# y by 32-feature blocks on quarters of the array, the state update on halves, and one chain for both power tables

## The chip, the cores and the metric

One Trainium2 chip, one of its cores. The metric is device time in microseconds (us), the median of three runs: 607.88 us before the change (607.52 to 608.14). Engines: PE is TensorE (PEld its weight loads), DVE is VectorE, ACT is ScalarE, POOL is GpSimd, SP is SyncE, whose queue issues the transfers (SPq).

## The reference

Two blocks after one another. The first is a linear attention with a decaying state, for each of 4 x 8 (batch, head) pairs over 768 steps with 48 features:

```
cur   = (u * k_t) outer v_t
y_t   = r_t @ (state + cur)
state = w * state + k_t outer v_t
```

The second takes y as x of 3072 tokens by 384 features (8 heads x 48) and computes `((x @ w1) * (x @ w2)) @ w3 @ w_out`, with w1, w2 of 384 x 1024, w3 of 1024 x 1024 and w_out of 1024 x 384. All is float32; the weights of the second block come as float64, as two 32-bit halves of a 64-bit word each.

## The kernel before

**Units and chunks.** Time is cut into 6 chunks of 128 steps (`c`), and with 4 batches (`b`) this gives 24 units `n`, four to a chunk. Inside a unit the step-by-step recurrence becomes matrices. `scale(n)` multiplies k and r on DVE by tables of powers of w (`pnk`, `pnr`, L290 and L291), so that r times k over the features gives all decays at once, and computes the diagonal (u k r) with L297 to L299; ACT writes it into `AT`. `turn(n)` transposes the scaled k and r on PE (L310), and ACT copies them out (L312). `pairs(n)` multiplies them, head by head on 64 rows of the array (L321), and DVE writes the part above the diagonal into `AT` (L324). `output(n)` computes y: from the second chunk on it adds the state's part (L365, one 128-column matmul for each pair of heads, heads padded from 48 to 64 features) and the chunk's own part (L369, one matmul for a head on 64 columns of the array). `update(n)` computes k outer v (L392, one matmul for two heads, of which the diagonal halves count) and DVE adds it to the state and decays it with the array `keep`, which is also zero outside the diagonal halves (L399 and L400; L402 in the first chunk). The last chunk has no update.

**Where y goes.** Four pairs of heads, padded to 64, fill 4 x 128 rows, and x has 3 x 128. The first three pairs are copied straight into `xT` (L376). The last pair is copied to `y` (L375), and six small transfers (L380) put its rows into the holes of the other three, 16 rows each. The rows of w1 and w2 are loaded in the order that this leaves (`spread`), four transfers a piece (L133).

**The second block.** w1 and w2 come in twelve pieces of 128 x 512, converted from float64: ACT takes the absolute value of the high word (`power`, L244), six DVE operations follow (L245 to L252). Three buffers `raw` go round. w3 and w_out are converted in the same way, and `fold(j)` multiplies them into `w34` beforehand (L276 to L281), so that per chunk there remain `ab(c, j)` for 8 blocks j (L416 into `ps_a`, ACT's copy L418, L421 into `ps_b`, DVE's product L422) and `o(c, b)` (L427, L430, a transfer out). A float32 matmul is two instructions on PE, a transpose one.

**What sets the order.** The program is written as steps: for each unit `scale(n+1)`, `pairs(n)`, `turn(n+1)`, `output(n)`, `update(n)`, and between them as many entries of the chunk's list `beside[c]` as are due (L487). The list for chunk 0 is the first half of the pieces of w1 and w2; for chunk 1 the second half, beside the projection of chunk 0; for chunk 2 w_out and w3 beside the projection of chunk 1. From these steps a scheduler forms one queue for each engine, in which instructions run strictly in order; so an instruction that waits holds all behind it on its engine. It may place work of neighbouring steps before or behind one another.

**The start.** The powers of w are built by doubling: `up` (for r) on DVE, `down` (for k) on POOL, both from `wucol`, which a transpose on PE makes from `wu` (L164). They are transposed (L228) and copied (L230) before the first `scale` can write k and r.

The whole program exists twice, in a fast arm and in one for decays outside 0.6 to 1.6 (L497); the inputs take the fast one.

## Time and profile before

| | |
|---|---|
| median of the runs | 607.88 us |
| the profiled execution: its time, and its span | 606.07 us, 604.2 us |
| mean granted clock of PE | 0.991 |
| busy: PE, DVE, ACT, POOL | 554.2, 261.5, 172.6, 10.3 us |
| transfers | 88916 packets, 38.62 MB |
| y into the holes (L380) | 144 transfers of 8 KB, landing after 1.8 us |

The page cuts the span into 40 slices of 15.1 us and gives the busy share of each in tenths, 9 being 90% or more. A share over the whole span says little here: the start waits for loads and tables, the stretch up to about 133 us has conversions on DVE beside the recurrence, and after that PE is hardly ever idle. So the stretches are read apart. In the chain of waits each piece begins where the one before it ends; where all pieces belong to PE, their lengths are the price of PE's work.

### The profile page before, as it was taken

The page shows a single profiled execution, that of the slowest core. Times are in us where ns is not written, and L with a number is a line of the kernel's source. Part 1 is how long each engine was busy: PE and PEld are TensorE (multiplying, and loading weights), DVE is VectorE, ACT ScalarE, POOL GpSimd, SP SyncE. Part 2 cuts the span into 40 slices and gives each one's busy share as a digit, 9 for nine tenths or more (in the row PEclk, how much of TensorE's full clock was granted, in tenths as well). Part 3 has the DMA queues.
Part 4 walks back from the last instruction along what each step waited for, and adds up shares of the span by engine and source line. Part 5 has one row for each costly group of instructions (what it writes and reads, how often), then busy time and mean ns, then how long its engine had stood idle before and what let it go on. Part 6 is the DMA issues. An engine that isn't in the chain of part 4 may idle for free.

```text
span 604.2 us, 6718 instructions
## 1 busy us (share of the span) xinstructions
PE 554.2 (92%) x2441; PEld 321.0 (53%) x2441; DVE 261.5 (43%) x497; ACT 172.6 (29%) x423; POOL 10.3 (2%) x36
## 2 busy tenths in 40 slices
PE   0298987679999999999999999999999999999996
PEld 0277445344556656656555565565555555554453
DVE  3896578489996667765103131313121101001100
ACT  2465233334444334334012122131332211111100
POOL 2400000000000000000000000000000000000000
PEclk9999999699999999999999999999999999999999
DMA  8534862733754233420211111102100000000001
GB/s 158 109 76 96 158 123 58 142 83 82 202 150 104 85 97 88 112 63 17 52 40 29 27 43 28 42 17 52 31 16 14 16 17 16 18 36 0 1 14 43
DMA packets 88916, 38.62 MB, mean 64 GB/s; under 512 B 78761, under 2 KB 84266, under 8 KB 88874
## 3 DMA queue, kind: packets, MB, share of 16 engines
q1 hardware_dynamic: 88874, 38.10, 26.8%
q8 instruction: 21, 0.34, 0.2%
q14 instruction: 21, 0.17, 0.1%
HBM read 32.18 MB, written 4.72 MB: 61 GB/s over the span
## 4 chain that ended last, share of the span: by engine, by line
PE 86%; DVE 5%; SPq 4%; DMA 2%; ACT 1%; issue 1%; DVEq 0%; ACTq 0%
PE ps_o L427 21%; PE ps_a L416 20%; PE ps_b L421 20%; PE ps_w L280 7%; PE ps_y L369 4%; PE ps_a L321 4%; PE ps_y L365 3%; PE ps_s L392 3%; PE ps_rT L310 2%; PE ps_kT L310 2%; DMA rin<-in_r_dram 1%; SPq L380 1%; PE ps_w3T L276 1%; SPq L133 1%; DMA raw<-in_moe_w_dram 1%
## 5 line engine op out<-in xcount | busy, mean ns | idle before, releaser
L416 PE MATMUL ps_a<-xT,w 128*128 128x512 f32 x288 | 133.9, 600 | 4.2 <-DVE w L252 4.2
L421 PE MATMUL ps_b<-xT,w 128*128 128x512 f32 x288 | 133.8, 598 | 3.4 <-DVE w L252 2.5
L427 PE MATMUL ps_o<-w,abt 128*128 128x384 f32 x384 | 128.0, 490 | 0.0
L422 DVE TENSOR_TENSOR abt<-ps_b,a 128x512 f32<-128x512 f32 x48 | 33.1, 690 | 186.1 <-PE ps_b L421 169.1
L427 PEld LDWEIGHTS ps_o<-w,abt 128*128 128x128 f32 x384 | 71.8, 190 | 49.6 <-issue 2.3
L421 PEld LDWEIGHTS ps_b<-xT,w 128*128 128x128 f32 x288 | 54.3, 191 | 71.6 <-issue 63.4
L416 PEld LDWEIGHTS ps_a<-xT,w 128*128 128x128 f32 x288 | 52.9, 191 | 61.6 <-issue 52.2
L418 ACT COPY a<-ps_a 128x512 f32<-128x512 f32 x48 | 28.0, 584 | 140.6 <-PE ps_a L416 137.7
L304 ACT ACTIVATE AT<-ident,dg 128x128 f32<-128x128 f32 x192 | 58.9, 394 | 6.8 <-DVE dg L299 6.8
L430 ACT COPY osb<-ps_o 128x384 f32<-128x384 f32 x24 | 11.5, 478 | 119.6 <-PE ps_o L427 107.8
L280 PE MATMUL ps_w<-wo,w3T 128*128 128x384 f32 x128 | 43.0, 489 | 0.6 <-ACT w3T L277 0.5
L324 DVE COPY_PREDICATED AT<-later,ps_a 128x512 f32<-128x512 int32 x48 | 32.3, 721 | 18.8 <-PE ps_a L321 17.9
L321 PEld LDWEIGHTS ps_a<-rT,kT 64*128 64x128 f32 x384 | 25.3, 195 | 16.5 <-issue 8.4
L321 PE MATMUL ps_a<-rT,kT 64*128 64x128 f32 x384 | 31.4, 298 | 2.8 <-ACT rT L312 2.8
L280 PEld LDWEIGHTS ps_w<-wo,w3T 128*128 128x128 f32 x128 | 23.7, 190 | 16.0 <-ACT w3T L277 1.0
L244 ACT ACTIVATE power<-raw 128x512 f32<-128x512 f32 (+1 forms) x36 | 23.4, 653 | 25.2 <-DVE t L251 19.4
L369 PE MATMUL ps_y<-AT,vnat 128*64 128x128 f32 x384 | 28.8, 280 | 0.9 <-ACT kT L312 0.6
L392 PE MATMUL ps_s<-vnat,ks 128*128 128x128 f32 x160 | 24.3, 286 | 0.0
L369 PEld LDWEIGHTS ps_y<-AT,vnat 128*64 128x64 f32 x384 | 21.6, 136 | 4.9 <-ACT kT L312 0.8
L312 ACT COPY kT<-ps_kT 128x512 f32<-128x512 f32 x24 | 14.0, 584 | 34.9 <-PE ps_kT L310 34.9
L251 DVE SCALAR_TENSOR_TENSOR t<-raw,power 128x512 f32<-128x512 uint32 (+1 forms) x36 | 23.6, 656 | 0.3
L299 DVE TENSOR_REDUCE dg<-ruk 128x8 f32<-128x384 f32 x24 | 13.1, 547 | 24.3 <-ACT AT L304 24.2
(74 smaller groups left out, 382.6 us busy)
## 6 DMA issues: line engine op xcount, KB each, us to landing
raw<-in_moe_w_dram SPq DMA_DIRECT2D x16, 512.0 KB, 4.1
kin<-in_k_dram SPq DMA_DIRECT2D x24, 192.0 KB, 3.6
rin<-in_r_dram SPq DMA_DIRECT2D x24, 192.0 KB, 3.6
vnat<-in_v_dram SPq DMA_DIRECT2D x24, 192.0 KB, 3.4
raw<-in_moe_w_dram SPq DMA_DIRECT2D x24, 192.0 KB, 3.7
out_dram<-osb SPq DMA_DIRECT2D x24, 192.0 KB, 1.9
raw<-in_moe_w_out_dram SPq DMA_DIRECT2D x8, 384.0 KB, 3.3
xT<-y SPq DMA_DIRECT2D x144, 8.0 KB, 1.8
```

The costliest lines, as they stand in the source:

```text
L280: nc.tensor.matmul(ps, lhsT=w3T[:, kc, :], rhs=wo[kc], start=(kc == 0), stop=(kc == KF - 1))
L304: nc.scalar.activation(out=AT[n][:, i, p, :], in_=ident, func=COPY, scale=dg[:, h:h + 1])
L310: nc.tensor.transpose(ps[:, p, :], src[n % NS][:, 2 * p:2 * p + 2, :].rearrange("t h d -> t (h d)"), ident)
L321: nc.tensor.matmul(ps[i][:, p, :], lhsT=kT[n][rows(i), p, :], rhs=rT[n][rows(i), p, :], start=True, stop=True)
L324: nc.vector.copy_predicated(AT[n][:, i], later.bitcast(I32)[:, None, :].to_broadcast([C, NP, C]), ps[i])
L369: nc.tensor.matmul(ps[rows(i), p], lhsT=vnat[n % NV][:, 2 * p + i, :], rhs=AT[n][:, i, p, :], start=not c, stop=True, skip_group_check=True)
L392: nc.tensor.matmul(ps[:, p], lhsT=kk[:, 2 * p:2 * p + 2, :].rearrange("t h d -> t (h d)"), rhs=vnat[n % NV][:, 2 * p:2 * p + 2, :], start= ...
L416: nc.tensor.matmul(pa, lhsT=w1[:, q, js], rhs=xT[c][:, q, :], start=(q == 0), stop=(q == KM - 1))
L418: nc.scalar.copy(out=a, in_=pa)
L421: nc.tensor.matmul(pb, lhsT=w2[:, q, js], rhs=xT[c][:, q, :], start=(q == 0), stop=(q == KM - 1))
L422: nc.vector.tensor_mul(abt[c, j], pb, a)
L427: nc.tensor.matmul(po, lhsT=abt[c, j][:, b * C:(b + 1) * C], rhs=w34[:, j, :], start=(j == 0), stop=(j == KF - 1))
```

## The change

- **y in blocks of 32.** The 96 features of a pair of heads are three blocks of 32, and the twelve blocks of the four pairs land, four to a 128-row group, in three groups: this is x's own order, so `spread`, the copy to `y` and the six transfers of L380 are gone, and a piece of w1 or w2 is one transfer. A block uses 32 columns of the array. The state's part has 12 such matmuls per unit, the chunk's own part 16: a middle block holds features of two heads and takes two.
- **State.** `st` has 96 columns for a pair instead of 128. Each head's k outer v is a matmul on 64 columns of the array with 48 columns of v, all on the head's own rows. DVE adds the two halves apart (64 partitions each), and the decay is one multiply by the column `wc`, repeated; `keep` is gone.
- **Order.** `pairs(n+1)` is computed in unit n, ahead of `output(n)` and `update(n)`. There are two steps to a unit instead of five: `scale` and `turn` of the next unit; `pairs` of the next, `output` and `update`. The entries of `beside` come between these two.
- **Tables.** One array `both` holds the powers for k and for r, built by one chain on DVE; the decay column is loaded by two transfers instead of a transpose on PE. k and r share one array (`krin`, `krs`), so `scale` multiplies both in one instruction. An ACT instruction on one element (`warm`) stands at the very start.
- **Pieces of w1 and w2** are taken alternately, w1 and w2, instead of three of w1 and then three of w2.

The core of the diff:

```diff
     ab_pieces = ...
-                 for z in range(DF // PIECE) for dst, src in ((w1, moe_w1), (w2, moe_w2)) for q in range(KM)]
+                 for js in (slice(z * PIECE, (z + 1) * PIECE) for z in range(DF // PIECE))
+                 for q in range(KM) for dst, src in ((w1, moe_w1), (w2, moe_w2))]
...
-            for to, of in parts:
-                nc.sync.dma_start(out=raw[to], in_=src[of, cols])
+        nc.sync.dma_start(out=raw, in_=src)
...
         def output(n):
             ps = psM.tile([P, NP, C], F32, tag="m", name=f"ps_y{n}")
+            blocks = [(p, j, divmod(3 * p + j, P // Q)) for p in range(NP) for j in range(3)]
+            to = lambda q, g: ps[g * Q:(g + 1) * Q, q, :]
             if c:
-                for p in range(NP):
-                    nc.tensor.matmul(ps[:, p], lhsT=st[b][:, p].rearrange("x i e -> x (i e)"), rhs=rw[:, p], ...)
-            for p in range(NP):
-                for i in range(2):
-                    nc.tensor.matmul(ps[rows(i), p], lhsT=vnat[n % NV][:, 2 * p + i, :], rhs=AT[n][:, i, p, :], ...)
-            y = work.tile([P, C], F32, tag="y", bufs=3, name=f"y{n}")
-            nc.scalar.copy(out=y, in_=ps[:, NP - 1, :])
-            nc.scalar.copy(out=xT[c][:, :, bs], in_=ps[:, 0:KM, :])
-            for i in range(2):
-                for q in range(KM):
-                    at = i * PAD + q * HOLE
-                    nc.sync.dma_start(out=xT[c][i * PAD + D:(i + 1) * PAD, q, bs], in_=y[at:at + HOLE, :])
+                for p, j, (q, g) in blocks:
+                    nc.tensor.matmul(to(q, g), lhsT=st[b][:, p, j * Q:(j + 1) * Q], rhs=rw[:, p], ...)
+            at = (0, Q, PAD + D - Q)
+            parts = [(p, j, at[j], j // 2, pos) for p, j, pos in blocks]
+            parts += [(p, j, D, 1, pos) for p, j, pos in blocks if j == 1]
+            vv = vnat[n % NV].rearrange("t (p i) d -> t p (i d)", i=2)
+            for m, (p, j, x, i, (q, g)) in enumerate(parts):
+                nc.tensor.matmul(to(q, g), lhsT=vv[:, p, x:x + Q], rhs=AT[n][:, i, p, :], ...)
+            nc.scalar.copy(out=xT[c][:, :, b * C:(b + 1) * C], in_=ps[:, 0:KM, :])
...
         def update(n):
-            for p in range(NP):
-                nc.tensor.matmul(ps[:, p], lhsT=kk[:, 2 * p:2 * p + 2, :].rearrange("t h d -> t (h d)"),
-                                 rhs=vnat[n % NV][:, 2 * p:2 * p + 2, :], start=True, stop=True)
-            if fast:
-                if c:
-                    nc.vector.tensor_add(old, new, old)
-                    nc.vector.tensor_mul(old, old, by)
+            for p in range(NP):
+                for i in range(2):
+                    nc.tensor.matmul(ps[rows(i), p, 0:D], lhsT=kk[:, 2 * p + i, :], rhs=vnat[n % NV][:, 2 * p + i, 0:D],
+                                     start=True, stop=True)
+            for i in range(2):
+                own = st[b][rows(i), :, i * D:(i + 1) * D]
+                if fast and not c:
+                    nc.vector.tensor_mul(own, ps[rows(i), :, 0:D], wc[rows(i)].to_broadcast([PAD, NP, D]))
+                else:
+                    nc.vector.tensor_add(own, ps[rows(i), :, 0:D], own)
+            if fast and c:
+                nc.vector.tensor_mul(st[b], st[b], wc.to_broadcast([P, NP, PD]))
...
-                if n + 1 < NU:
-                    steps.append(lambda: scale(n + 1))
-                steps.append(lambda: pairs(n))
-                if n + 1 < NU:
-                    steps.append(lambda: turn(n + 1))
-                steps += [lambda: output(n), lambda: update(n)]
+                if n + 1 < NU:
+                    steps += [lambda: (scale(n + 1), turn(n + 1))]
+                steps += [lambda: (n + 1 < NU and pairs(n + 1), output(n), update(n))]
```

**PE, a unit of the third chunk.** Before, around y and update of unit 11 (the number behind a name is the scheduler's; a row is one matmul or, with x, so many):

```order
L416 MATMUL ps_a_6_1572<-xT_681,w_93 128x512 x3
L421 MATMUL ps_b_6_1578<-xT_681,w_94 128x512 x3
L310 MATMUL ps_kT_1583<-ident,ks_75 128x128 x4
L310 MATMUL ps_rT_1590<-ident,rs_77 128x128 x4
L365 MATMUL ps_y_1608<-rT_1430,st_85 128x128 x4
L369 MATMUL ps_y_1608<-AT_1364,vnat_74 64x128 x8
L392 MATMUL ps_s_1640<-vnat_74,ks_76 128x128 x4
L416 MATMUL ps_a_7_1648<-xT_681,w_93 128x512 x3
L421 MATMUL ps_b_7_1654<-xT_681,w_94 128x512 x3
```

After, around y and update of unit 9 (L299 the pairs, L347 and L355 y, L373 the update, L395 and L400 the projections, L287 the transposes):

```order
L299 MATMUL ps_a_0_1298<-rT_1262,kT_1255 128x128
L299 MATMUL ps_a_1_1299<-rT_1262,kT_1255 128x128
L347 MATMUL ps_y_1310<-rT_1107,st_78 32x128 x12
L355 MATMUL ps_y_1310<-AT_1086,vnat_69 32x128 x16
L373 MATMUL ps_s_1340<-vnat_69,krs_73 64x48 x8
L395 MATMUL ps_a_3_1364<-xT_659,w_91 128x512 x3
L400 MATMUL ps_b_3_1370<-xT_659,w_92 128x512 x3
L287 MATMUL ps_kT_1404<-ident,krs_73 128x128 x4
L287 MATMUL ps_rT_1411<-ident,krs_73 128x128 x4
```

The pairs of the next unit now stand directly ahead of y, and the update directly behind it; before, the pairs stand apart from y.

**ACT, in the second chunk**, where the second half of w1 and w2 is converted (`raw` in turn for pieces 9 to 12). Before:

```order
L244 ACTIVATE power<-raw_81 128x512
L375 COPY y_1029<-ps_y_1016 128x128
L376 COPY xT_681<-ps_y_1016 128x3x128
L418 COPY a_4_971<-ps_a_4_967 128x512
L244 ACTIVATE power<-raw_79 128x512
L312 COPY kT_995<-ps_kT_990 128x512
L312 COPY rT_1002<-ps_rT_997 128x512
L304 ACTIVATE AT_957<-ident,dg_953 128x128 x8
L418 COPY a_5_1009<-ps_a_5_1005 128x512
L244 ACTIVATE power<-raw_80 128x512
L375 COPY y_1162<-ps_y_1148 128x128
L244 ACTIVATE power<-raw_81 128x512
```

After, the last three of the twelve pieces:

```order
L223 ACTIVATE power<-raw_74 128x512
L397 COPY a_2_818<-ps_a_2_814 128x512
L223 ACTIVATE power<-raw_75 128x512
L359 COPY xT_659<-ps_y_879 128x3x128
L290 COPY kT_848<-ps_kT_843 128x512
L290 COPY rT_855<-ps_rT_850 128x512
L281 ACTIVATE AT_834<-ident,dg_830 128x128 x8
L223 ACTIVATE power<-raw_76 128x512
L397 COPY a_3_926<-ps_a_3_922 128x512
L397 COPY a_4_980<-ps_a_4_976 128x512
```

Before, three powers stand behind the copies of a_4 and a_5, which need the second half of w1; after, all stand ahead of the copy of a_4.

**DVE, from the first chunk to the second.** Before, where the fifth conversion begins (L245; L324 with AT_513 and AT_608 is the pairs of units 4 and 5):

```order
L324 COPY_PREDICATED AT_513<-later,ps_a_0_617 128x512
L298 TENSOR_TENSOR ruk_603<-ruk_603,ub 128x384
L324 COPY_PREDICATED AT_513<-later,ps_a_1_618 128x512
L299 TENSOR_REDUCE dg_604<-ruk_603 128x8
L399 TENSOR_TENSOR st_82<-ps_s_691,st_82 128x512
L400 TENSOR_TENSOR st_82<-st_82,keep 128x512
L324 COPY_PREDICATED AT_608<-later,ps_a_0_742 128x512
L324 COPY_PREDICATED AT_608<-later,ps_a_1_743 128x512
L245 SCALAR_TENSOR_TENSOR w_94<-power,raw_80 128x512
```

After, where the fifth and the sixth begin (L224; L302 with AT_492 is the pairs of unit 4):

```order
L224 SCALAR_TENSOR_TENSOR w_91<-power,raw_75 128x512
L380 TENSOR_TENSOR st_80<-ps_s_555,wn 64x4x48
L226 TENSOR_SCALAR t<-w_91 128x512
L380 TENSOR_TENSOR st_80<-ps_s_555,wn 64x4x48
L227 SCALAR_TENSOR_TENSOR w_91<-w_91,t 128x512
L269 TENSOR_TENSOR krs_73<-krin_68,pn 128x16x48
L229 TENSOR_SCALAR power<-w_91 128x512
L224 SCALAR_TENSOR_TENSOR w_92<-power,raw_76 128x512
L230 SCALAR_TENSOR_TENSOR t<-raw_75,power 128x512
L302 COPY_PREDICATED AT_492<-later,ps_a_0_525 128x512
```

The sixth conversion now begins before the pairs of unit 4; before, the fifth began behind those of unit 5.

## Rows read from the trace of the kernel before

**Rows 1.** The page: busy time by engine, and tenths in 40 slices.
```profile
PE 554.2 (92%) x2441; PEld 321.0 (53%) x2441; DVE 261.5 (43%) x497; ACT 172.6 (29%) x423; POOL 10.3 (2%) x36
...
PE   0298987679999999999999999999999999999996
...
PEclk9999999699999999999999999999999999999999
```
**Rows 2.** Busy time by stretch, with the granted clock and the transfers.
```profile
core 0: us, PE busy (x) PEld busy (x) DVE busy (x) ACT busy (x) POOL busy (x), PEclk, DMA share, GB/s
...
26.00:56.00 30.00, 25.34 (x225) 20.38 (x226) 25.27 (x48) 15.96 (x44) 0.00 (x0) 1.00 0.41 84
56.00:133.00 77.00, 61.85 (x334) 36.46 (x333) 52.38 (x94) 25.89 (x64) 0.00 (x0) 0.93 0.51 105
133.00:250.00 117.00, 115.58 (x499) 65.50 (x498) 93.76 (x186) 48.33 (x113) 0.00 (x0) 1.00 0.47 122
250.00:604.00 354.00, 349.23 (x1379) 196.93 (x1377) 75.64 (x125) 73.58 (x180) 0.00 (x0) 1.00 0.11 28
```
**Rows 3.** Who waited for whom, 56 to 133 us: us in total, times, longest.
```profile
DVE w L245 <- DMA raw<-in_moe_w_dram: 7.4, 2, 5.0
DVE AT L324 <- PE ps_a L321: 6.1, 1, 6.1
...
PE ps_a L416 <- DVE w L252: 4.2, 1, 4.2
...
PE ps_b L421 <- DVE w L252: 2.5, 3, 1.4
```
**Rows 4.** ACT in order of time: start, us, instruction [idle before <-releaser].
```profile
108.43 0.59 ACT L418 COPY a<-ps_a 128x512 f32<-128x512 f32 x1 [4.69 <-PE ps_a L416]
108.91 0.67 ACT L244 ACTIVATE power<-raw 128x512 f32<-128x512 f32 x1
```
**Rows 5.** SyncE's queue in order of time: start, us, issues.
```profile
85.56 1.71 SPq L133 DMA_DIRECT2D raw<-in_moe_w_dram  x4
...
96.85 1.72 SPq L133 DMA_DIRECT2D raw<-in_moe_w_dram  x4
98.67 4.40 SPq L380 DMA_DIRECT2D xT<-y  x6
106.50 1.71 SPq L133 DMA_DIRECT2D raw<-in_moe_w_dram  x4
```
**Rows 6.** The chain that ended last, steady part: start us, us, what.
```profile
348.06 0.89 PE ps_y L365 x8
348.95 1.02 PE ps_y L369 x16
349.97 5.36 PE ps_o L427 x16
355.33 0.89 PE ps_s L392 x8
...
361.37 1.09 PE ps_a L321 x16
...
516.82 20.64 PE ps_o L427 x64
```
**Rows 7.** DVE groups by line and shape: busy us, mean ns | idle before.
```profile
L297 DVE TENSOR_TENSOR ruk<-kin,rin 128x384 f32<-128x384 f32 x24 | 13.3, 554 | 21.6 <-DMA kin<-in_k_dram 15.2 <-DMA rin<-in_r_dram 6.3
...
L399 DVE TENSOR_TENSOR st<-ps_s,st 128x512 f32<-128x512 f32 x16 | 11.0, 689 | 22.3 <-PE ps_s L392 22.0
...
L400 DVE TENSOR_TENSOR st<-st,keep 128x512 f32<-128x512 f32 x16 | 11.0, 685 | 0.1
```
**Rows 8.** PE at the start, in order of time.
```profile
22.61 1.09 PE L228 MATMUL ps_pk<-ident,down 128*128 128x128 f32 x4 [18.31 <-POOL down L205]
...
27.83 1.12 PE L310 MATMUL ps_kT<-ident,ks 128*128 128x128 f32 x4 [3.28 <-DVE ks L290]
```

More of the change, by code (lines that the diff above doesn't have):

```diff
@@ L158 @@
                             skip_runtime_bounds_check_because="a comparison's result is 0 or 1")
-    wucol = const.tile([P, 2 * NP, 1], F32)
-    with tc.tile_pool(name="psW", bufs=1, space=PSUM) as psW:
-        ps = psW.tile([P, 2 * NP], F32, name="ps_wu")
-        nc.tensor.transpose(ps, wu.rearrange("a i d -> a (i d)"), ident[0:2 * NP, 0:2 * NP])
-        nc.vector.tensor_copy(out=wucol.rearrange("x a o -> x (a o)"), in_=ps)
     def program(fast):
@@ L177, in body @@
         psF = arm.enter_context(tc.tile_pool(name="psF", bufs=2, space=PSUM))
-        wn = tab.tile([P, LEVELS + 1, NP, 1], F32)
-        keep = tab.tile([P, NP, 2, PAD], F32)
-        pn = {}
+        for t in st:
+            nc.gpsimd.memset(t, 0.0)
         if fast:
-            nc.vector.tensor_scalar(wn[:, 0], wucol[:, 0:NP, :], W_LOW, W_HIGH, ALU.max, ALU.min)
-        else:
-            nc.vector.tensor_copy(out=wn[:, 0], in_=wucol[:, 0:NP, :])
-        for l in range(LEVELS):
-            nc.vector.tensor_mul(wn[:, l + 1], wn[:, l], wn[:, l])
@@ new lines, in body @@
+            wn = tab.tile([P, LEVELS + 1, 3 * NP, 1], F32)
+            nc.vector.tensor_scalar(wn[:, 0, 0:NP, :], wucol, W_LOW, W_HIGH, ALU.max, ALU.min)
+            for l in range(LEVELS):
+                nc.vector.tensor_mul(wn[:, l + 1, 0:NP, :], wn[:, l, 0:NP, :], wn[:, l, 0:NP, :])
+            nc.vector.reciprocal(wn[:, 0:LEVELS, NP:2 * NP, :], wn[:, 0:LEVELS, 0:NP, :])
+            nc.vector.tensor_copy(out=wn[:, 0:LEVELS, 2 * NP:, :], in_=wn[:, 0:LEVELS, 0:NP, :])
+            both = tab.tile([P, 2, NP, C], F32)
@@ L215, in body @@
+            natural = [both[:, g] for g in range(2)]
+        else:
+            wn = tab.tile([P, LEVELS + 1, NP, 1], F32)
+            nc.vector.tensor_copy(out=wn[:, 0], in_=wucol)
             pw = tab.tile([P, NP, C], F32)
@@ L267, in w3_weight @@
             js = slice(z * PIECE, (z + 1) * PIECE)
[L268 removed]
+            weight((w3n[j][:, js], moe_w3[j * P:(j + 1) * P, js]))
         def fold(j):
@@ L364, in output @@
-                for p in range(NP):
-                    nc.tensor.matmul(ps[:, p], lhsT=st[b][:, p].rearrange("x i e -> x (i e)"), rhs=rw[:, p],
-                                     start=(p == 0), stop=False, skip_group_check=True)
-            for p in range(NP):
-                for i in range(2):
-                    nc.tensor.matmul(ps[rows(i), p], lhsT=vnat[n % NV][:, 2 * p + i, :], rhs=AT[n][:, i, p, :],
-                                     start=not c, stop=True, skip_group_check=True)
+                for p, j, (q, g) in blocks:
+                    nc.tensor.matmul(to(q, g), lhsT=st[b][:, p, j * Q:(j + 1) * Q], rhs=rw[:, p],
+                                     start=(q == 0), stop=False, skip_group_check=True)
@@ new lines, in output @@
+            at = (0, Q, PAD + D - Q)
[3 more added lines that the diff above has]
+            for m, (p, j, x, i, (q, g)) in enumerate(parts):
+                nc.tensor.matmul(to(q, g), lhsT=vv[:, p, x:x + Q], rhs=AT[n][:, i, p, :],
+                                 start=(not c and m < P // Q), stop=True, skip_group_check=True)
@@ L472, in body @@
         turn(0)
+        pairs(0)
         for c in range(NCH):
```

140 lines of the change are left out of this document (57 added, 83 removed).

## The prediction

> **What bounds the kernel now.** I read the page first. TensorE is busy for 92% of the span, and its row of tenths shows where it is not: three slices at the start, and the slices around 100 to 135 us; the clock row has its one low digit there [rows 1]. The table of stages puts numbers on it: from 133 us on PE is busy for 115.58 of 117.00 us and 349.23 of 354.00, so there every microsecond of PE work is a microsecond of span; between 56 and 133 us it is busy for 61.85 of 77.00, at a mean granted clock of 0.93, while VectorE has 52.38 [rows 2]. So the change has two prices: PE work after 133 us, and waits before it.
>
> Next the waits between 56 and 133 us. PE waits longest for a converted weight piece (L252, 4.2 and 2.5 us), and DVE waits 7.4 us in front of L245 "for the raw weights" and 6.1 us for the pairs on PE [rows 3]. For the shorter of these two waits (7.4 - 5.0 = 2.4 us) the load is not to blame: three raw buffers go round, and the piece whose power is taken at 108.91 was issued at 85.56, before the loads at 96.85 and 106.50 for the two pieces behind it [rows 4, 5]. ScalarE shows the link that came last: the copy of the projection's result out of PSUM (L418) waits 4.69 us for PE and runs at 108.43, and the power of the weight piece (L244), queued behind it, starts at 108.91 [rows 4]. That is a ring: PE waits for DVE, DVE for ACT's power, that power for a copy, and the copy for PE. SyncE's queue is the second brake: six small DMAs per unit (L380) hold it for 4.40 us, behind them wait the loads of weights and of k, r, v [rows 5].
>
> Last the chain of waits in the steady part, where one unit's pieces stand with nothing between them [rows 6].
>
> **The change, part by part.** All sums are made against the profiled execution (606.07 us, of which 604.2 are span); the median of the runs is 1.81 us above it, and I add that difference again at the end.
>
> *y on quarters.* Eight whole-array instructions take 0.89 us (L365, L392), so one slot of 128 columns costs 0.111 us. The 16 half-array instructions of L321 take 1.09 us, and the work behind a visit to array parts is 0.20 us longer than it need be (5.36 us for 16 ps_o against 20.64/4 = 5.16) [rows 6]. Taking the same 0.20 off the entry of L321 leaves 0.89 us for 16 halves: two halves share one slot. Before, y costs 8 + 16/2 = 16 slots, 1.78 us per unit. After, it is 12 + 16 = 28 matmuls of two passes, 56 quarter instructions. If four share a slot as two halves do, that is 14 slots, 1.56 us (-0.22); if only two are ever beside each other, 56 x 0.0556 = 3.11 us (+1.33). The trace has no quarter. The nearest row is L321's, where every part of the array that exists is used; I take 1.60 (-0.18) and keep both ends.
>
> *State update on halves.* Four matmuls of 128 columns (0.89 us with their two passes, L392 [rows 6]) become eight on half arrays, 48 columns each: 16 instructions, two at a time. At the price of a half it stays 8 slots, 0.89 us; if it goes with the columns, 48/128 of that, 0.33. I take the middle, 0.60 (-0.29).
>
> *One visit.* Two visits per unit now cost 0.13 in (1.02 - 0.89, L369) and 0.20 out, 0.20 in (L321) and 0.20 out: 0.73 us [rows 6]. In the new order the pairs, y and the update follow one another, so PE enters and leaves once, 0.40, and changes its parts twice within. These inner changes are free at best (-0.33) and cost 0.20 each at worst (+0.07); as every change of parts in the rows costs 0.13 to 0.20, I take 0.15 each: -0.03. The Trainium skill, TensorEngine Tiling (Array Packing), section Key Properties, says that changing the tiling mode, and not only the tile, drains TensorE: by it 64-row to 32-column to 64-column are drains too, and "one visit" as such saves next to nothing. The trace's 0.13 to 0.20 us agrees for the changes from and to the whole array; the inner ones no run shows yet.
>
> Together -0.50 us for a unit with an update and -0.21 without. From 133 us on there are twelve and four of them: 6.0 + 0.8 = 6.8 us.
>
> *The front, 26 to 133 us.* DVE is busy for 25.27 + 52.38 = 77.7 of these 107 us [rows 2], and ten of the twelve conversions of w1 and w2 lie in it. The merged scale and the smaller update (two adds on 64 partitions at some 0.29 and one multiply at 0.55 for 0.69 + 0.69 [rows 7], estimates from the elements) take about 2 us off. Without a wait DVE would be through at 26 + 76 = 102 us; that is one bound (31 us gained). PE has 61.85 us of work from 56 us on, less about 2 for four units and 2 for the clock: it can't stand where it now stands at 133 before 56 + 58 = 114; that is the binding bound, 19 us. The other end is no gain at all. What speaks for most of it: in the new order ACT computes the power of all twelve pieces ahead of the copy of a_4, the first result that needs the second half of the weights, so the ring is cut; the 6 x 24 DMAs of L380 are gone, and a raw piece is one issue in place of four; and the six pieces that the first half of the projection needs stand inside chunk 0 on DVE, in place of four and a bit. I take 16 of the 19. What is late next is DVE: in 133 to 250 us it is busy for 93.76 of 117.00 us [rows 2], so a PE that comes 16 us early meets w_out and w3 conversions ahead of the scale of the next units; I price that at 4 us (bounds 0 and 16). Net 12 us.
>
> *At nothing:* the start. The power table of k ends on POOL and PE waits 18.31 us for it; then another 3.28 us pass until the first scaled k, because DVE does a weight piece between [rows 8]. In the new order one DVE chain makes both tables, with the same loads in front and again conversion steps in between; the early table load on ACT and one DMA for the decay column in place of a transpose are hidden behind these loads. It could be 1.5 us better or worse. The removed copies of y (L375) lie beside PE.
>
> Sum: 6.8 + 12 = 18.8 us off; 606.07 - 18.8 = 587.3, and with the 1.81 us to the median **589 us**.
>
> **Rivals.**
> 1. *Quarters run only two at a time* (slower). The two passes of a matmul go to the same quarter; if PE starts them in order and looks one ahead, two are beside each other, as in L321. Then y is 3.11 us: +1.33 - 0.29 - 0.03 = +1.01 per unit, 12.1 us for twelve, 5.2 for the last four, and the front keeps 12 - 4 x 1.5 = 6: 607.9 + 17.3 - 6 = 619 us. It decides below 2.5 quarters to a slot: 56 x 0.111 / 2.5 = 2.49 us, 0.89 more than I count, is over 20 units 17.8 of the 18.8 us. Against it: halves already use all that there is, two of two.
> 2. *Three at a time.* y is 56 x 0.111 / 3 = 2.07 us, +0.29, which the update gives back: steady part 0.7 us worse, front 12 - 4 x 0.47 = 10: 598.6 us. The Trainium skill, TensorE: Matmul & The Clock Gate, section Measured speedup vs the span model, has three column tiles at 2.38 times one; by that share four quarters would be 3.2 at a time, some 597 us. The trace shows 2.0 for two, no more.
> 3. *The front stays.* The waits of rows 3 change their names: PE in order behind pairs that are now computed a unit ahead, or DVE behind two more conversions in chunk 0. Then 6.8 and some 2 us of chunk 1 are left: 599 us. For it: DVE is the fuller engine until 250 us. Against: the ring on ACT is cut by order, not by luck.
> 4. *The front is gained whole* and the inner changes are free: 19 + 6.8 + 16 x 0.3 = 30 us, 578 us.
>
> **Chances.** Forecast 0.52 (its own range 582 to 596), rival 1 0.13, rival 2 0.13, rival 3 0.14, rival 4 0.08. The range takes in rivals 2 to 4 and part of the way to rival 1: 577 to 607. A change under 0.2% (1.2 us) can't be told from none. Faster: all but rival 1 and a little of rival 3, 0.82; slower 0.15; same 0.03.
>
> **What would show it.** Right: in the chain of the steady part y takes about 1.6 us for its 56 instructions, groups starting in fours; the update about 0.6; the extra on the work behind a visit appears once per unit; between 56 and 133 us PE is busy for over 90%, and the wait of L416 for a converted piece is short. Wrong: quarter instructions of 0.055 us apiece (rival 1), a wait of the scale or the transposes of units 8 to 11 for DVE of more than 5 us, or an idle PE around 100 us as now (rival 3).

## The result and the profile after

The changed kernel takes 569.23 us (569.16 to 569.48, four runs) beside 608.01 us for the kernel before: a ratio of 0.9364, 95% interval 0.9348 to 0.938. That is 38.8 us off. The forecast was 18.8 us off, 589 us, in a range of 577 to 607: the direction was right, the time lies below the range, and the gain is twice what was forecast.

The page of the kernel after: busy time by engine, then PE and its clock in 40 slices of 14.2 us, as in [rows 1].

```profile
PE 534.4 (94%) x3304; PEld 304.8 (54%) x3304; DVE 254.9 (45%) x495; ACT 169.2 (30%) x400; POOL 3.5 (1%) x17
...
PE   0388999999999999999999999999999999999996
...
PEclk9999999999999999999999999999999999999998
```

The holes around 100 to 135 us are gone, and with them the low clock digit. The profiled execution (569.27 us) has a span of 567.8 us, 36.4 less than before. PE's busy time fell by 554.2 - 534.4 = 19.8 us, its idle time by the other 16.6 (604.2 - 554.2 = 50.0 to 567.8 - 534.4 = 33.4).

The stages of the kernel after, with the columns of [rows 2]:

```profile
26.00:56.00 30.00, 25.47 (x351) 19.32 (x349) 28.57 (x54) 18.22 (x45) 0.00 (x0) 1.00 0.69 161
56.00:133.00 77.00, 76.90 (x578) 42.14 (x578) 76.38 (x158) 35.78 (x88) 0.00 (x0) 1.00 0.51 134
133.00:250.00 117.00, 116.58 (x842) 69.80 (x841) 83.37 (x155) 47.16 (x108) 0.00 (x0) 1.00 0.31 86
250.00:567.80 317.80, 312.66 (x1527) 171.18 (x1525) 52.14 (x83) 59.41 (x137) 0.00 (x0) 1.00 0.10 26
```

From 56 to 133 us PE is busy for 76.90 of 77.00 us at full clock, where it had 61.85 at 0.93, and DVE for 76.38 where it had 52.38. Behind it, from 133 to 250 us, DVE has less left to do (83.37 for 93.76), so nothing is given back. The waits of PE from 26 to 133 us (in total, times, longest; here the longest two) lie before 56 us; the 4.2 us for a converted piece and the 2.5 of [rows 3] have no successor:

```profile
PE ps_y L355 <- DVE AT L302: 1.5, 3, 1.1
PE ps_y L355 <- ACT AT L281: 1.3, 1, 1.3
```

How much earlier the front ends is read on PE at the first product of the fold (w_out with w3). Before:

```profile
179.80 2.42 PE L280 MATMUL ps_w<-wo,w3T 128*128 128x384 f32 x7
```

and after:

```profile
154.03 2.20 PE L259 MATMUL ps_w<-wo,w3T 128*128 128x384 f32 x6
```

25.8 us. The rest of the 36.4, 10.6 us, comes behind it, in the steady part, whose chain reads (start, us, what; compare [rows 6]):

```profile
280.62 1.09 PE ps_a L299 x16
281.71 0.79 PE ps_y L347 x24
282.50 0.87 PE ps_y L355 x32
283.37 0.60 PE ps_s L373 x16
283.98 2.77 PE ps_a L395 x6
286.75 2.58 PE ps_b L400 x6
```

The pairs cost what they did. y is 0.79 + 0.87 = 1.66 us for 56 quarter instructions, the update 0.61 with the gap behind it, and the whole-array work behind pays 2.77 - 2.58 = 0.19. One unit before: 0.89 + 1.02 + 0.20 + 0.89 + 1.09 + 0.20 = 4.29 us; after: 1.09 + 1.66 + 0.61 + 0.19 = 3.55. That is 0.74 less, and 0.46 less in a unit without update. For the twelve and four units that the prediction counts this makes 12 x 0.74 + 4 x 0.46 = 10.7 us. That it is next to the 10.6 is luck, for the two rows of the fold don't stand behind the same work: in the kernel after, PE has computed one unit more when it comes to the fold (the updates of eleven units, before of ten), some 3.5 us of work. At equal work 25.8 + 3.5 = 29.3 us come ahead of the fold and 7.1 behind it; the thirteen units left there, nine of them with an update, make 9 x 0.74 + 4 x 0.46 = 8.5, 1.4 more than that.

### The profile page after: what moved, and what is told of

It reads as the page before. It is cut to its first block, busy times and chain, and to the rows that moved or that the text cites. A ratio compares the mean times of both kernels' runs of the same rounds, so it can differ in the third digit from the quotient of the medians.

```text
span 567.8 us, 8077 instructions
## 1 busy us (share of the span) xinstructions
PE 534.4 (94%) x3304; PEld 304.8 (54%) x3304; DVE 254.9 (45%) x495; ACT 169.2 (30%) x400; POOL 3.5 (1%) x17
## 3 DMA queue, kind: packets, MB, share of 16 engines
q1 hardware_dynamic: 84082, 36.91, 25.0%
## 4 chain that ended last, share of the span: by engine, by line
PE 87%; DVE 7%; SPq 2%; issue 1%; ACT 1%; DMA 1%; ACTq 0%; DVEq 0%
PE ps_o L406 22%; PE ps_b L400 21%; PE ps_a L395 20%; PE ps_w L259 7%; PE ps_a L299 4%; PE ps_y L355 3%; PE ps_y L347 3%; PE ps_kT L287 2%; PE ps_s L373 2%; PE ps_rT L287 1%; PE ps_w3T L255 1%; SPq L109 1%; DMA krin<-in_r_dram 1%; DVE krs L269 1%; DVE AT L302 1%
## 5 line engine op out<-in xcount | busy, mean ns | idle before, releaser
L395 PE MATMUL ps_a<-xT,w 128*128 128x512 f32 x288 | 133.2, 597 | 0.0
L400 PE MATMUL ps_b<-xT,w 128*128 128x512 f32 x288 | 132.1, 593 | 0.1
L400 PEld LDWEIGHTS ps_b<-xT,w 128*128 128x128 f32 x288 | 54.4, 190 | 68.9 <-issue 64.3
L395 PEld LDWEIGHTS ps_a<-xT,w 128*128 128x128 f32 x288 | 53.1, 190 | 56.6 <-issue 50.9
L302 DVE COPY_PREDICATED AT<-later,ps_a 128x512 f32<-128x512 int32 x48 | 32.9, 731 | 30.7 <-PE ps_a L299 30.3
L299 PEld LDWEIGHTS ps_a<-rT,kT 64*128 64x128 f32 x384 | 25.4, 190 | 16.4 <-issue 9.4
L359 ACT COPY xT<-ps_y 128x384 f32<-128x384 f32 x24 | 11.4, 476 | 73.7 <-PE ps_y L355 73.5
L299 PE MATMUL ps_a<-rT,kT 64*128 64x128 f32 x384 | 30.7, 289 | 1.2 <-ACT rT L290 0.8
L355 PE MATMUL ps_y<-AT,vnat 128*32 128x128 f32 x768 | 28.3, 274 | 2.9 <-DVE AT L302 1.5
L355 PEld LDWEIGHTS ps_y<-AT,vnat 128*32 128x32 f32 x768 | 22.4, 110 | 4.5 <-DVE AT L302 2.5
L269 DVE TENSOR_TENSOR krs<-krin,pn 128x768 f32<-128x768 f32 x24 | 22.9, 957 | 0.6
```

What stands on the lines that cost most here:

```text
L269: nc.vector.tensor_mul(krs[n % NS][:, :, :, :D], kr, pn[:, :, :, :D])
L299: nc.tensor.matmul(ps[i][:, p, :], lhsT=kT[n][rows(i), p, :], rhs=rT[n][rows(i), p, :], start=True, stop=True)
L302: nc.vector.copy_predicated(AT[n][:, i], later.bitcast(I32)[:, None, :].to_broadcast([C, NP, C]), ps[i])
L355: nc.tensor.matmul(to(q, g), lhsT=vv[:, p, x:x + Q], rhs=AT[n][:, i, p, :], start=(not c and m < P // Q), stop=True, skip_group_check=True)
L395: nc.tensor.matmul(pa, lhsT=w1[:, q, js], rhs=xT[c][:, q, :], start=(q == 0), stop=(q == KM - 1))
L400: nc.tensor.matmul(pb, lhsT=w2[:, q, js], rhs=xT[c][:, q, :], start=(q == 0), stop=(q == KM - 1))
```

## The experiments

Theory Q: the front is held by SyncE's queue, in which the six small transfers of each unit and the four issues of each piece stand in order. Its rivals: the new order of steps (S), and the smaller work on PE and DVE (W).

**Run 1: after, with the five steps of before.**

```diff
-                    steps += [lambda: (scale(n + 1), turn(n + 1))]
-                steps += [lambda: (n + 1 < NU and pairs(n + 1), output(n), update(n))]
+                    steps.append(lambda: scale(n + 1))
+                steps.append(lambda: pairs(n))
+                if n + 1 < NU:
+                    steps.append(lambda: turn(n + 1))
+                steps += [lambda: output(n), lambda: update(n)]
```

> The changed kernel with the old five steps to a unit (scale, pairs of this unit, turn, output, update, with the projection's work between all of them). Theory S (the new order of steps freed the front): the waits between 56 and 133 us come back, PE is idle there for 10 us or more, 584 to 590 us. Theory Q (the transfers taken out of SyncE's queue freed it, and with them the scheduler placed ACT's powers early): the front stays, PE busy over 95% from 56 to 133 us; only the visits to array parts rise from 34 to 58, each unit some 0.2 us dearer: 573 to 576 us.

Measured 576.85 us (ratio 0.9504, 0.9479 to 0.953), 7.6 above after and just over Q's range. PE is busy for 540.6 us, 6.2 more, and idle for 34.2, 0.8 more: the new steps save PE's busy time (it goes to array parts 34 times instead of 58), not waits. From 56 to 133 us it is busy for 75.49 of 77.00 us: the front is free without them.

**Run 4: before, with the steps of after.**

```diff
-                    steps.append(lambda: scale(n + 1))
-                steps.append(lambda: pairs(n))
-                ...
-                steps += [lambda: output(n), lambda: update(n)]
+                    steps += [lambda: (scale(n + 1), turn(n + 1))]
+                steps += [lambda: (n + 1 < NU and pairs(n + 1), output(n), update(n))]
```

> The kernel before, with the new order of steps alone (pairs of the next unit ahead of output and update, two steps to a unit). Theory S: the front is freed, 585 to 592 us. Theory Q: the front's waits stay (ACT's powers still stand behind the copies of a_4 and a_5), only some exits from array parts go: 600 to 607 us.

606.61 us (0.9968, 0.9936 to 1.0001): no difference. S falls.

**Run 5: before, with the queue freed.**

```diff
-            y = work.tile([P, C], F32, tag="y", bufs=3, name=f"y{n}")
-            nc.scalar.copy(out=y, in_=ps[:, NP - 1, :])
-            ... nc.sync.dma_start(out=xT[c][i * PAD + D:(i + 1) * PAD, q, bs], in_=y[at:at + HOLE, :])   (x6)
     def spread(q):
-        ... four parts
+        return [(slice(0, P), slice(q * P, (q + 1) * P))]
```

> The kernel before with SyncE's queue freed and nothing else: the copy of pair 3's y and the six small transfers of each unit (L380) left out, and a piece of w1 or w2 loaded by one transfer instead of four (so the rows of pair 3 are missing from x, and the weights' rows are not in x's order: the output isn't the reference's). y stays on halves, the update on the whole array, the old steps. Theory Q (the queue held the front): after's front without its cheaper y, update and start; e1 shows 31.2 us with old steps, of these some 10.5 are the steady part, 2.6 the start and 2 the front's own cheaper PE work, so 16 are left: 590 to 594 us, PE busy over 90% of 56 to 133 us. Rival W (the front came from less work on PE and DVE in chunk 0, by merged scale, smaller update, quarters): 602 to 608 us, PE still near 62 us busy in 56 to 133.

578.93 us (0.9524, 0.947 to 0.9579): 28.4 us off, nearly twice what Q had expected, and W falls. PE runs the same 2441 instructions as before. The page's first row and three stages:

```profile
PE 546.2 (95%) x2441; PEld 318.2 (55%) x2441; DVE 258.0 (45%) x497; ACT 168.3 (29%) x399; POOL 9.9 (2%) x36
```

```profile
26.00:56.00 30.00, 28.57 (x236) 21.78 (x237) 27.93 (x53) 18.34 (x45) 0.00 (x0) 1.00 0.70 160
56.00:133.00 77.00, 77.00 (x392) 43.74 (x391) 77.00 (x159) 34.97 (x86) 0.00 (x0) 1.00 0.52 137
133.00:250.00 117.00, 116.45 (x563) 71.12 (x562) 81.81 (x147) 44.41 (x101) 0.00 (x0) 1.00 0.32 84
```

Span 576.9, 27.3 less than before: 19.3 us of idle time (50.0 to 30.7) and 8.0 us of busy time on the same instructions (554.2 to 546.2). PE and DVE are both full from 56 to 133 us. The first product of the fold runs at 151.89 us, 27.9 earlier than in the kernel before (179.80), with the same instructions ahead of it on PE: the whole gain lies in the front. With the six transfers the edit also takes their copy off ACT (L375, 24 times 0.27 us) and the projection no longer waits for them; run 6 keeps both. SyncE's queue shows what changed (start, us that the issues took, what). Before:

```profile
31.00 1.27 SPq L133 DMA_DIRECT2D raw<-in_moe_w_dram  x2
36.44 3.77 SPq L380 DMA_DIRECT2D xT<-y  x6
40.31 1.44 SPq L101 DMA_DIRECT2D vnat<-in_v_dram  x1
41.84 3.69 SPq L380 DMA_DIRECT2D xT<-y  x6
45.63 0.53 SPq L101 DMA_DIRECT2D vnat<-in_v_dram  x1
46.67 3.67 SPq L380 DMA_DIRECT2D xT<-y  x6
...
52.50 3.49 SPq L133 DMA_DIRECT2D raw<-in_moe_w_dram  x4
```

and in run 5:

```profile
29.90 0.65 SPq L124 DMA_DIRECT2D raw<-in_moe_w_dram  x1
...
35.97 0.53 SPq L124 DMA_DIRECT2D raw<-in_moe_w_dram  x1
...
43.02 0.34 SPq L124 DMA_DIRECT2D raw<-in_moe_w_dram  x1
```

The fifth piece is loaded at 29.90 (52.50 before), the seventh at 43.02: no block of six issues that must wait for y of its unit stands ahead of it.

**Run 6: before, with the pieces in one transfer; the six transfers stay.**

```diff
     def spread(q):
-        ... four parts
+        return [(slice(0, P), slice(q * P, (q + 1) * P))]
```

> The kernel before with the 12 pieces of w1 and w2 loaded by one transfer each instead of four (their rows then not in x's order, the output isn't the reference's); the six small transfers per unit stay. Theory Q4 (the 48 issues of the piece loads are what counts): nearly e5, 591 to 597 us. Theory Q6 (the 144 small transfers count, in whose shadow the loads stand): 603 to 608 us. Both alike: 598 to 603 us.

585.87 us (0.9633, 0.9562 to 0.9704): 21.4 of the 28.4 us come by the 36 issues less for twelve pieces, and 6.9 more when the 144 small transfers go too (run 5). Q4, and more of it than expected. What the small transfers alone give, with four issues to a piece left, was not run in the kernel before.

**Run 8: after, with the six small transfers.**

```diff
+            y = work.tile([P, C], F32, tag="y", bufs=3, name=f"y{n}")
+            nc.scalar.copy(out=y, in_=ps[:, KM - 1, :])
+            ... nc.sync.dma_start(out=z[i * PAD + D:(i + 1) * PAD, q, :], in_=y[at:at + 16, :])   (x6)
```

> The kernel after with only the six small transfers per unit back (a copy of 128x128 on ACT and six transfers into a tile that nobody reads). ACT's powers keep after's places. Theory Q4: 569 to 575 us, the transfers cost only what they delay k, r, v. Theory Q6: 600 to 640 us.

576.32 us (0.9484, 0.9429 to 0.954): 7.1 above after, the mirror of the 6.9, a little over Q4's range.

**Runs 2 and 7: after, with pieces in four transfers, with and without the small ones.**

```diff
-        nc.sync.dma_start(out=raw, in_=src)
+        for at, to in ((0, 48), (48, 64), (64, 112), (112, 128)):
+            nc.sync.dma_start(out=raw[at:to], in_=src[at:to])
```

> The changed kernel with the old load on SyncE's queue: each weight piece in four transfers again, and per unit one more copy on ACT and six small transfers into a scratch tile that nothing reads. Theory Q: the front's waits come back, PE idle by 10 us or more between 56 and 133 us, 582 to 592 us. Theory S: the transfers are hidden as long as PE has work, at most 572 us.

> The kernel after with only the 12 piece loads in four transfers each (36 issues more, some 16 us of SyncE by 0.43 us each). Theory Q4: most of e2's 74.6 us come back, 610 to 635 us, since in the program's order on ACT the powers of the w3 pieces then also fall behind the copies of the projection. Theory Q6: 569 to 576 us.

643.8 us (1.0607, 1.0574 to 1.064) and 590.79 us (0.9711, 0.9656 to 0.9767). Both miss, and both edits were heavier than their expectations say: they split all 36 pieces, w3 and w_out too, where the kernel before splits twelve. So they show that a longer queue costs more, slower than before even, but not the size for twelve. Nor do the two parts add: the issues alone cost 21.6 us (run 7), the small transfers alone 7.1 (run 8), both together 74.6 (run 2).

**Run 9: after, with the queue of before.**

```diff
-        nc.sync.dma_start(out=raw, in_=src)
+        for at, to in ((0, 48), (48, 64), (64, 112), (112, 128)) if any(piece is x for x in ab_pieces) else ((0, P),):
+            nc.sync.dma_start(out=raw[at:to], in_=src[at:to])
+            ... and the copy and six transfers of run 8
```

> The kernel after with exactly the queue of the kernel before: the 12 pieces of w1 and w2 in four transfers each (the second and the seventh run split all 36 pieces, w3 and w_out too, so they say more than was meant), and the six small transfers with the copy on ACT. Theory Q (the queue is the front, whatever else changed): the 28.4 us of the fifth run come back, 590 to 603 us. Rival O (the new order is more sensitive to the queue than the old one, as the second run's 643.8 us suggests): over 620 us. Rival N (the new order needs the queue less): under 582 us.

602.78 us (0.9904, 0.9876 to 0.9932): 33.6 us come back, 26.5 of them over run 8 by the 36 issues. (Unlike before, w1 and w2 still take turns, and nothing reads what the small transfers write.) From 56 to 133 us its row is like before's again, low clock and all:

```profile
56.00:133.00 77.00, 57.75 (x475) 30.89 (x474) 48.92 (x89) 25.68 (x65) 0.00 (x0) 0.91 0.52 101
```

Its idle time (599.3 - 546.6 = 52.7) is 19.3 over after's, the same 19.3 that run 5 took away. The queue is thus shown from both sides; everything else in the change is worth 1% while the old queue stands, and 9.7 us once it is free (578.93 in run 5, 569.23 after).

**Run 3: after, with the update on the whole array.**

```diff
-                for i in range(2):
-                    nc.tensor.matmul(ps[rows(i), p, 0:D], lhsT=kk[:, 2 * p + i, :], rhs=vnat[n % NV][:, 2 * p + i, 0:D], ...)
+                nc.tensor.matmul(ps[:, p], lhsT=kk[:, 2 * p:2 * p + 2, :]..., rhs=vnat[n % NV][:, 2 * p:2 * p + 2, :]..., ...)
```

> The changed kernel with the state update on the whole array again (four matmuls of 128 columns for two heads each; the diagonal halves are added). If the halves are what makes the update cheap (0.61 us with the change of parts, against 0.89 and an exit of 0.20 before it): 20 units x 0.28 us more, 574 to 576 us. If the 48 columns gain nothing and only the visit counts: within 1 us of the changed kernel.

573.75 us (0.9445), 4.5 over after; PE is busy for 539.0, 4.6 more. Over 20 units that is 0.23 us each for the halves.

**Run 10: after, with y's blocks sorted by quarter.**

```diff
-            blocks = [(p, j, divmod(3 * p + j, P // Q)) for p in range(NP) for j in range(3)]
+            blocks = sorted([...], key=lambda t: t[2][1])
...
```

> The kernel after with the blocks of y sorted by quarter, so that the matmuls of one quarter follow one another, three or four blocks of two passes each. If TensorE starts its instructions in order and neighbours must lie in different quarters: 56 x 0.111 = 6.2 us for y less the overlap at the changes, some +3.9 us for 20 units and +2.4 for four, 640 to 660 us. If it sorts them into quarters by itself: 568 to 573 us. If the four-fold share in y is not real and the whole gain lies elsewhere: also 568 to 573, but with y's time in the chain unchanged near 1.66 us.

591.14 us (0.9718, 0.9687 to 0.9749), between the two. The chain of one unit:

```profile
292.66 1.09 PE ps_a L299 x16
293.75 1.19 PE ps_y L347 x20
294.94 0.03 PE ps_y L355
294.97 0.08 PE ps_y L347 x2
...
295.27 1.21 PE ps_y L355 x28
296.48 0.60 PE ps_s L373 x16
```

y is 296.48 - 293.75 = 2.73 us, 1.07 more, which over 20 units is 21.4 of the 21.9. So the order over the quarters is what makes y 1.66, and four do run at once in after: 32 instructions in 0.87 us are 0.027 each, a quarter of a slot of 0.111; at that price the other 24 take 0.65 of their 0.79, and 0.14 is the entry into quarters. But sorted, it is still 0.049 each and not 0.11: within a quarter the records start 0.110 us apart, and the next quarter's first instruction starts 0.248 us after the first one of the quarter before, whose last three of six start only behind it. So, by these records, PE does not hold up a later instruction for another quarter behind them: in the chain L355 starts ahead of the last of L347, which stand before it in the program. To that extent PE's queue is not strictly in order.

**Runs 13 and 14: the power of the twelve pieces on DVE, in before and in run 9's kernel.** Run 5 leaves open how the queue costs its 28 us.

```diff
-            nc.scalar.activation(out=power, in_=hi.bitcast(F32), func=ABS)
+            if src is moe_w1 or src is moe_w2:
+                nc.vector.tensor_scalar(pb, hi, 0x7FFFFFFF, None, ALU.bitwise_and)
+            else: ...
```

> The kernel before with its queue and its steps as they are; only the power of the 12 pieces of w1 and w2 (|high word|, L244) is taken by VectorE, in front of its own conversion, and no longer by ScalarE. DVE gets 12 x 0.42 to 0.69 us more. Theory P (the pieces have landed; their power stands on ACT behind a copy that waits for PE): the ring is cut, and most of the 28.4 us of the fifth run come, less some 7 us of DVE: 583 to 594 us, PE busy for over 70 of the 77 us from 56 to 133. Theory L (the queue brings the pieces late): 603 to 612 us, DVE then waits for the transfers themselves.

> The ninth run's kernel (after with the queue of before, 602.8 us) with the power of the 12 pieces on VectorE. Theory P: 574 to 586 us. Theory L: 598 to 606 us.

606.75 us (0.9975, 0.9942 to 1.0007) and 599.36 us (0.9871, 0.9848 to 0.9894; 3.4 under run 9, which these intervals don't tell apart). Theory P misses. The times lie in L's ranges, but not by L's mechanism: no wait of DVE for a transfer of weights shows from 56 to 133 us in run 13. DVE in order of time shows where the ring went:

```profile
114.99 0.41 DVE L245 TENSOR_SCALAR power<-raw 128x512 uint32<-128x512 uint32 x1
122.37 0.73 DVE L327 COPY_PREDICATED AT<-later,ps_a 128x512 f32<-128x512 int32 x1 [6.96 <-ACT a L421]
122.99 0.68 DVE L248 SCALAR_TENSOR_TENSOR w<-power,raw 128x512 f32<-128x512 f32 x1
```

The power is there at 115.4, but the conversion that uses it stands on DVE behind a copy of the pairs that comes 7 us later.

**Runs 16 to 18: the place of the conversions, the queue left alone.**

```diff
-            W12[0],
-            merge(W12[1], AB(0, range(KH))) + AB(0, range(KH, KF)),
+            W12[0] + W12[1][:4],                                        (run 16; run 17: W12[0] + W12[1])
+            merge(W12[1][4:], AB(0, range(KH))) + AB(0, range(KH, KF)),
```

and in after, for run 18, `W12[0][:3]` in chunk 0 and the other three ahead of chunk 1's list.

> The kernel before with its queue and its steps; only the list beside the chunks is changed: four of the six conversions of the second half of w1 and w2 stand in chunk 0's list instead of chunk 1's. On DVE the fifth piece then stands ahead of unit 5's part of AT and no longer behind unit 6's, the tenth piece ahead of the first product of the projection, no longer behind the fourth. Theory D (in the kernel before the pieces lie landed for 7 to 20 us, and their place in DVE's and ACT's order holds them): the front shrinks with the queue as it is, 585 to 598 us. Theory L (the transfers themselves are late): DVE now waits for them in front of the units' work, 603 to 620 us.

> As the run before, with all six of them in chunk 0's list. Theory D: 583 to 598 us, a little below the run before if the units don't starve. Theory L: 606 to 625 us, above the run before.

> The kernel after, its queue free, with three of chunk 0's six conversions put at the head of chunk 1's list: on DVE the fifth piece moves from ahead of unit 5's AT to behind it, the sixth behind unit 6's. Theory D: 573 to 582 us. Theory L: within 2 us of after, 568 to 571 us.

600.24 us (0.9858, 0.9826 to 0.9891), 604.76 us (0.9945, 0.9919 to 0.9971) and 567.58 us (0.9325). The place alone gives 8.2 us of the 28, and a further move loses half of that again. Runs 16 and 17 lie between the ranges of D and L, run 18 just under L's. The queue of run 16 shows why the place is not enough:

```profile
29.13 1.50 SPq L133 DMA_DIRECT2D raw<-in_moe_w_dram  x3
36.34 3.77 SPq L380 DMA_DIRECT2D xT<-y  x6
40.21 1.19 SPq L101 DMA_DIRECT2D vnat<-in_v_dram  x1
41.45 0.58 SPq L133 DMA_DIRECT2D raw<-in_moe_w_dram  x1
42.13 3.68 SPq L380 DMA_DIRECT2D xT<-y  x6
45.85 1.04 SPq L133 DMA_DIRECT2D raw<-in_moe_w_dram  x2
```

The four issues of the fifth piece run from 30.27 (the last of the three at 29.13) to 46.89: two blocks of L380 stand between them. The first must wait for the y of its unit, the second only takes its 3.7 us of issue. Among the waits of SyncE's queue from 26 to 133 us (in total, times, longest) the first is

```profile
SPq L380 <- ACT AT L304: 6.2, 1, 6.2
```

After's queue has no such block, and there moving three conversions back costs nothing: run 18 (567.58 us) is no slower than after.

**Runs 11, 12 and 15: the start.** In after, the table chain on DVE stands behind a product r*u*k that waits for its loads.

```diff
-            nc.vector.tensor_mul(ruk, kr[:, 0], kr[:, 1])
-            nc.vector.tensor_mul(ruk, ruk, ub)
+            eng = nc.gpsimd if n < 2 else nc.vector          (run 15: n < 6)
+            eng.tensor_mul(ruk, kr[:, 0], kr[:, 1])
+            eng.tensor_mul(ruk, ruk, ub)
```

and in runs 12 and 15 the loads of v of units 0 and 1 are issued behind the first and second piece.

> The kernel after with the two products r*u*k of units 0 and 1 on POOL instead of VectorE. In after, DVE waits from 6.8 to 12.9 us for r of unit 1 in front of the product, and the table chain stands behind it; PE starts at 21.5 us. If that in-order wait is what holds the start: the first table on PE at 16 to 19 us, and as PE and DVE are both full until 133 us the gain is kept: 563 to 567 us. If the first weight piece (its power is taken at about 15 us) holds the chain in the same way: PE at 20 to 21.5 us and 568 to 570 us.

> As the run before, and the loads of v of units 0 and 1 issued behind the first and the second weight piece (in after each stands ahead of it, and the second takes 4.6 us to issue). If the first weight piece is what is late next: 2 to 4 us below the run before, 560 to 564 us. If the order of these loads doesn't matter: equal to it within 1 us; if y of unit 0 now waits for v: 1 to 3 us above.

> The twelfth run's kernel (567.0 us) with the products of units 0 to 5 on POOL instead of 0 and 1: DVE, busy for 28.7 of the 30 us from 26 to 56, gets rid of 4 x 2 x 0.55 = 4.4 us there. If DVE bounds this stretch: 563 to 566 us. If the pieces of weights or the clock of TensorE bound it: 566.5 to 568 us. If POOL's 2.1 us per unit come late for the diagonal (AT): 568 to 571 us.

567.72 us (0.9328), 567.02 us (0.9319) and 566.46 us (0.9324, 0.9304 to 0.9344; four runs from 566.32 to 566.67). The wait that was meant is gone: PE's first wait, 21.5 us in after, is

```profile
PE ps_p L210 <- DVE both L187: 16.1, 1, 16.1
```

in run 11. Of these 5.4 us 1.5 are kept. In the profiled execution (568.88 us, the slowest of its four) PE is then ahead of DVE and ACT: its idle time falls by only 4.1 (33.4 to 29.3), and its busy time grows by 3.3 (534.4 to 537.7), with a low clock in this stretch:

```profile
36.00:40.00 4.00, 2.88 (x56) 2.20 (x52) 3.84 (x9) 2.19 (x7) 0.00 (x0) 1.00 0.60 136
40.00:44.00 4.00, 2.74 (x24) 2.31 (x24) 3.97 (x9) 3.46 (x10) 0.00 (x0) 0.82 0.92 180
44.00:48.00 4.00, 3.72 (x48) 2.48 (x46) 2.36 (x4) 2.18 (x7) 0.00 (x0) 0.50 0.52 152
```

Run 12, with the v loads moved, keeps 1.00 there; its median is 0.7 us below run 11's, its profiled span 2.2 (564.8 for 567.0):

```profile
36.00:40.00 4.00, 2.18 (x41) 1.67 (x32) 3.87 (x8) 2.90 (x10) 0.00 (x0) 1.00 0.63 127
40.00:44.00 4.00, 2.39 (x26) 1.86 (x28) 3.97 (x9) 3.48 (x10) 0.00 (x0) 1.00 0.87 175
44.00:48.00 4.00, 4.00 (x88) 3.18 (x88) 3.40 (x8) 2.54 (x7) 0.00 (x0) 1.00 0.60 168
```

Run 15 is the fastest measured, 2.8 us under after. Over run 12 it gains 0.6 us by the medians and nothing by the ratios (0.9324 and 0.9319); its clock from 26 to 56 us is 0.89 again.

## Why the prediction was wrong, step by step

**The front: the step that failed.** The prediction took 16 us and gave 4 back; 25.8 us came by the first fold, 29.3 at equal work, and the freed queue alone gives 27.9 there (run 5). Three parts of that step were wrong.

- *The bound.* "It can't stand where it now stands at 133 before 56 + 58 = 114; that is the binding bound, 19 us" took two things as fixed: where PE stands at 56 us, and all but 2 us of the clock's cost. Neither is. Run 5 frees the queue and takes away 19.3 us of idle time, some of it before 56 us (PE is busy for 28.57 us from 26 to 56 there, for 25.34 before), and 8.0 us of busy time on the same instructions. The low clock was written in [rows 2] as 0.93 over 77 us. It lies in two neighbouring stretches of the kernel before, behind the 4.2 us wait for a piece (what share of the 8.0 it has, no run splits):

```profile
105.00:115.00 10.00, 4.12 (x16) 2.52 (x18) 7.41 (x15) 2.32 (x4) 0.00 (x0) 0.67 0.64 115
115.00:125.00 10.00, 9.92 (x53) 5.62 (x50) 3.77 (x8) 4.11 (x12) 0.00 (x0) 0.82 0.43 99
```

- *The 4 us given back* never came. What DVE does before 133 us it need not do after: 76.38 us in place of 52.38 before it, 83.37 in place of 93.76 behind.
- *The cause.* The prediction put the ring on ACT first ("the ring is cut" by "the new order") and called SyncE's queue "the second brake". It is the other way round: the new steps alone give nothing that can be measured (run 4), nor does the power off ACT (run 13); the freed queue gives 28.4 us (run 5). The sentences on the queue, that loads of weights and of k, r, v wait behind the six small transfers and that a piece is one issue in place of four, were right and stood without a price of their own.

How the queue's 28 us come about is settled in part. Taken out of the kernel before one after the other, the pieces' issues give 21.4 us and the small transfers 6.9 more (runs 6 and 5); put into the kernel after, the small transfers cost 7.1 and the issues 26.5 more (runs 8 and 9). Since the two don't add in run 2, these shares hold for this order alone. The trace of the kernel before tells late transfers from late places. The fifth piece is late by its transfer: its issue ends at 55.99 us, and its power runs at 60.81. The pieces behind it are not. From the end of their issue to their power 11 to 23 us pass, of which a transfer takes 3.4 to 3.7 (a whole piece in run 5 takes 4.2, so the transfers themselves are not slower in parts). The sixth, at the 5.0 us wait that [rows 3] put down to the load, is issued by 62.14, and its power stands on ACT behind a copy that waits for PE:

```profile
72.47 0.58 ACT L418 COPY a<-ps_a 128x512 f32<-128x512 f32 x1 [4.77 <-PE ps_a L416]
72.95 0.67 ACT L244 ACTIVATE power<-raw 128x512 f32<-128x512 f32 x1
```

So the ring that the prediction saw is there, and it goes when the queue is freed: in run 5 PE is busy for all of the 77.00 us. Moving the conversions forward without touching the queue gives 8.2 us (run 16), moving more of them gives less (run 17), and no other places were tried. How much of the rest is the late fifth piece, and how much is other instructions that stand elsewhere in the order of DVE and ACT since the build reckons with other transfers, no run separates: freeing the queue changes both at once, and no kernel here holds one of them still.

**The steady part: the mechanism was right, one size was off.** Forecast -0.50 us for a unit with update and 6.8 us for twelve and four units; measured -0.74, which makes 10.7 for as many. (Behind 133 us the kernel before has eleven and four, so the count was one too high.) *y*: taken as 1.60, measured 1.66 with the entry into quarters; less the 0.14 of the entry it is 1.52, next to the 1.56 of four to a slot. Rivals 1 and 2 (619 and 598.6 us) are out. *The update*: taken as 0.60, measured 0.60 with the change of parts ahead of it. In the records its pairs of instructions start 0.058 us apart, which for eight pairs is 0.46, between the bounds 0.33 and 0.89; the change is the other 0.14. *The visit*: -0.03 was forecast, with 0.15 us for each inner change on top of an update of 0.60; as the 0.60 has that change in it, it was counted twice. Run 3 finds 0.23 us a unit for the halves, a little under the 0.29 forecast. The two inner changes cost 0.14 us each. That agrees with the rule of the Trainium skill, TensorEngine Tiling (Array Packing), Key Properties, that changing the tiling mode drains TensorE. Four quarters take 0.027 us for an instruction where a whole-array slot takes 0.111, 4 times one. The Trainium skill, TensorE: Matmul & The Clock Gate, Measured speedup vs the span model, has 2.38 times for three column tiles; the estimate of 3.2 for four by that share does not hold here.

**At nothing: the start.** The first transposes of k run at 25.19 us where they ran at 27.83: 2.6 us better, outside the 1.5 either way. Runs 11 to 15 show that an in-order wait on DVE still holds 5.4 us there, of which 2.8 can be had.

**The sum.** 25.8 to the first fold and 10.6 behind it, or 29.3 and 7.1 at equal work: 36.4 us of span. Rival 4 (578 us) came nearest, with its whole front of 19 and free inner changes; the true front lies beyond its bound.

## What to carry to other kernels

A count of issues on an in-order queue deserves a price of its own: here 36 issues and 144 small transfers were worth 28 us, though they hardly add bytes (38.10 MB on the queue before, 36.91 in run 5); a block of six takes 3.7 to 4.4 us to issue, its first may wait for a result, and everything behind it waits along. A bound for a stretch must not take its own first line as fixed: work, waits and clock of the stretch ahead move with the same cause. And an isolated edit from both sides (freed in the kernel before, put back into the kernel after) told in two runs what no reading of the waits had. Rows of two kernels that are to divide a gain must have the same work ahead of them.

## What the runs showed of the hardware

- Four quarters of 32 columns run fully beside each other on float32 work, 0.027 us for a quarter instruction on 128 columns of data, where one on the whole array takes 0.111; and PE reaches past three waiting instructions of one quarter to start the next quarter's (run 10).
- On the way into quarters, and from quarters to halves, 0.14 us each go; back to the whole array 0.19.
- PE's clock fell to 0.50 of 2.4 GHz, its 1.2 GHz level, for one stretch of run 11 after PE had been busy for 2.88 and 2.74 of 4.00 us; in run 12, at 2.18 and 2.39 of the same 4.00 us, it stayed at full. Of an earlier start of 5.4 and 6.1 us the profiled executions keep 0.8 and 3.0. Why the one fell and not the other stays open.
